# A long convolution and two expert layers: the expert matmuls read their moving columns in another order, and the weights start 48 bytes later

## The chip, the cores and the metric

The kernel runs on one core of one Trainium2 chip. What is measured is the device time of one execution in microseconds (us); of several executions the median is given. The engines are named as in the profile: PE is TensorE's matmuls, PEld its weight loads, DVE is VectorE, ACT is ScalarE, POOL is GpSimd, SP is SyncE, which starts most DMAs.

## The reference

What is computed is a gated long convolution followed by two expert layers, one after the other, over 2 x 12480 = 24960 tokens of 128 features:

```python
h_filt = (np.maximum(pos_emb @ w1, 0.0) @ w2) * np.exp(-0.01 * pos)[:, None]
u = x * v
y = np.fft.irfft(np.fft.rfft(u, n=L, axis=1) * np.fft.rfft(h_filt, n=L, axis=0), n=L, axis=1)[:, :S, :]
x = (x * y).reshape(B * S, D)            # D = 128
h = x @ w_in;   x = (h * np.cos(h)) @ w_out                      # first expert, d_ff = 2048
h = x @ w_in2;  return (h * np.clip(h + 3.0, 0.0, 6.0) / 6.0) @ w_out2   # second expert, d_ff = 2048
```

Inputs are float32, the expert weights arrive as float64 bits and are split in the kernel into a high and a low float32r part.

## The kernel before, in words

`conv_phase` (until about 545 us) computes the convolution as matrix products for the transform of length 111 x 113, two features at a time (64 groups), and writes the product x * y to DRAM scratch. Its matmuls are float32 (L280 and L281, two at a time, in the left and right columns of the array). Beside it `decode` turns the weights into their two parts, 512 columns at a time.

`moe_phase` (from there to the end) holds the tokens as columns. There are 49 tiles (`TILES`): 47 of 512 tokens, and a first and a last one of 448. For each tile and expert there are 8 units; a unit is 256 of the 2048 hidden features.

- `front` (L685 to L703) multiplies a unit's two blocks of 128 x 128 input weights with the tile's 512 columns. Values are split in two float32r parts, so each block takes three matmuls: high weights on the high part `xh`, high weights on the low part `xl`, low weights on `xh`. It makes 6 matmuls, into PSUM tiles `ha0` and `ha1` (first expert, one buffer) or `hb` (second expert, two buffers).
- `m1_reduce`, `m1_gate` and `m1_split` (first expert) bring h into range (ACT L710, DVE L711), take the cosine and multiply (ACT L720, DVE L721) and split the product into `hi` (ACT L728) and `lo` (POOL L733). `m2_gate` and `m2_split` (second expert) do the same with ACT L740, DVE L741 and L755, POOL L758.
- `back` (L760 to L783) multiplies the unit's two 128 x 128 blocks of output weights with `hi` and `lo`: 6 matmuls that add to `acc`, a PSUM tile that is open over the tile's 8 units. After the eighth, ACT L777 and DVE L778 split `acc` into `x2h` and `x2l`, the second expert's input; or ACT L782 copies it to `o`, and SP writes `o` to the output.

The order is written out by hand in the loop at L795: iteration p takes front(p) of the first expert, then back of an earlier unit of the first, then front of the second expert 12 iterations behind, then back of an earlier unit of the second. In the middle of the kernel an iteration is thus 24 matmuls, each with a weight load of its own. In all there are 2 x 2 x 6 x 8 x 49 = 9408 such matmuls (6 in front, 6 in back, two experts).

Every matmul of `front` and `back` takes its columns in the order in which they lie (L701 and L769, `rhs=r[:, :n]`), and all tiles that they read start at multiples of 64 bytes. Weights are the first 4096 floats of a tile per matrix (`weights`, L78), 2048 high and then 2048 low.

Of the kernel before, what the change touches and what calls it, by code (L numbers as in the profile page):

```python
# [10 lines left out]
F32R = mybir.dt.float32r  # L11
INT32 = mybir.dt.int32
UINT32 = mybir.dt.uint32
ACTF = mybir.ActivationFunctionType
ALU = mybir.AluOpType
# [13 lines left out]
MP = 2 * M2  # L29
# [4 lines left out]
DFF = 2048  # L34
# [2 lines left out]
TT = 512  # L37
XW = 4 * N2
LINE = 64
HB = -(-max(36 * MP, 2 * DFF) // LINE) * LINE  # L40
XB = -(-XW // LINE) * LINE
TILES = [(TT + TOK % TT) // 2] + [TT] * (TOK // TT - 1) + [(TT + TOK % TT) // 2]
TWO_PI = 2.0 * np.pi
# [3 lines left out]
def kernel(  # L47
# [19 lines left out]
    nc = tc.nc  # L67
    dram = ctx.enter_context(tc.tile_pool(name="dram", bufs=1, space=DRAM))
    wp = ctx.enter_context(tc.tile_pool(name="wp", bufs=1))
# [6 lines left out]
    hq = ctx.enter_context(tc.tile_pool(name="hq", bufs=1))  # L76

    def weights(e, nm):  # L78
        if (nm, e) not in w_hi:
            if e == 0:  # L80
                t = wp.tile([128, 2, DFF], F32R, name=f"w{nm}")
            else:
                t = hq.tile([128, HB], F32R, tag=f"h{'io'.index(nm)}", name=f"v{nm}")[:, :2 * DFF]
                t = t.rearrange("p (z f) -> p z f", f=DFF)
            w_hi[nm, e], w_lo[nm, e] = t[:, 0, :], t[:, 1, :]
        return w_hi[nm, e], w_lo[nm, e]

# [23 lines left out]
    def decode(task, st, pool, lane):  # L111
        e, nm, c = task
        lo, hi = st[:, :, 0], st[:, :, 1]
        ex = pool.tile([128, DC], INT32, tag=f"wex{lane}", name="wex")
        mh = pool.tile([128, DC], INT32, tag=f"wmh{lane}", name="wmh")
        m = mh.bitcast(FP32)
        wh, wl = (w[:, c:c + DC] for w in weights(e, nm))
        nc.vector.tensor_scalar(ex, hi, 9, 0x3FFFFF, op0=ALU.logical_shift_right, op1=ALU.bitwise_and)
        nc.vector.tensor_scalar(mh, hi, 0x1FF, None, op0=ALU.bitwise_and)
        yield  # L120
        nc.scalar.activation(out=ex, in_=ex, func=ACTF.Relu, bias=b_exp, scale=-1.0)
        nc.scalar.activation(out=ex, in_=ex, func=ACTF.Relu, bias=b_max, scale=-(2.0 ** 12))
        nc.scalar.activation(out=m, in_=mh, func=ACTF.Copy, scale=2.0 ** -20)
        yield
        nc.vector.scalar_tensor_tensor(
            out=ex, in0=hi, scalar=-0x80000000, in1=ex, op0=ALU.bitwise_and, op1=ALU.bitwise_or
        )
        yield
        nc.scalar.copy(wh, ex.bitcast(FP32))
        nc.vector.scalar_tensor_tensor(  # L130
            out=m, in0=lo.bitcast(UINT32), scalar=2.0 ** -52, in1=m, op0=ALU.mult, op1=ALU.add
        )
        yield
        nc.vector.tensor_scalar(ex, ex, -0x800000, None, op0=ALU.bitwise_and)
        yield
        nc.gpsimd.tensor_tensor(out=wl, in0=m, in1=ex.bitcast(FP32), op=ALU.mult)
# [497 lines left out]
    def moe_phase(mctx):  # L634
# [14 lines left out]
        acc = {}  # L649

        def n_of(t):
            return TILES[t]
# [15 lines left out]
        def split_x(t):  # L668
# [10 lines left out]
            eng.tensor_tensor(out=lo[:, :n], in0=f[:, :n], in1=hi[:, :n], op=ALU.subtract)  # L679
            xs[0, t] = (hi, lo)  # L680

        class Unit:
            pass

        def front(e, t, u, split):  # L685
            n = n_of(t)
            un = Unit()
            un.e, un.t, un.u, un.n = e, t, u, n
            xh, xl = xs[e, t]
            if split:  # L690
                hs = [ps_a.tile([128, 1, TT], FP32, tag=f"ha{c}", name=f"ha{c}") for c in range(2)]
                un.parts = [(slice(c, c + 1), hs[c][:, :, :n]) for c in range(2)]
            else:
                h = ps_b.tile([128, 2, TT], FP32, tag="hb", name="hb")
                hs = [h[:, c:c + 1] for c in range(2)]
                un.parts = [(slice(0, 2), h[:, :, :n])]
            for c in range(2):
                sl = slice((2 * u + c) * 128, (2 * u + c + 1) * 128)
                for k, (w, r) in enumerate(((w_hi, xh), (w_hi, xl), (w_lo, xh))):
                    nc.tensor.matmul(  # L700
                        out=hs[c][:, 0, :n], lhsT=w["i", e][:, sl], rhs=r[:, :n], start=(k == 0), stop=(k == 2)  # L701
                    )
            return un  # L703

# [55 lines left out]
        def back(un):  # L760
            e, t, u, n = un.e, un.t, un.u, un.n
            if u == 0:
                bank = 1 if t == 0 else e
                acc[e] = ps_o.tile([128, TT], FP32, tag=f"acc{bank}", name=f"acc{e}")
            for k, (w, r) in enumerate(((w_hi, un.hi), (w_lo, un.hi), (w_hi, un.lo))):
                for c in range(2):
                    sl = slice((2 * u + c) * 128, (2 * u + c + 1) * 128)
                    nc.tensor.matmul(  # L768
                        out=acc[e][:, :n], lhsT=w["o", e][:, sl], rhs=r[:, c, :n],  # L769
                        start=(u == 0 and c == 0 and k == 0), stop=(u == KFF // 2 - 1 and c == 1 and k == 2),  # L770
                    )
            if u == KFF // 2 - 1:
                a = acc[e][:, :n]
                if e == 0:
                    hi = x2_p.tile([128, TT], F32R, tag="x2h", name="x2h")
                    lo = x2_p.tile([128, TT], F32R, tag="x2l", name="x2l")
                    nc.scalar.copy(hi[:, :n], a)  # L777
                    nc.vector.tensor_tensor(out=lo[:, :n], in0=a, in1=hi[:, :n], op=ALU.subtract)  # L778
                    xs[1, t] = (hi, lo)
                else:  # L780
                    o = o_p.tile([128, TT], FP32, tag="o", name="o")
                    nc.scalar.activation(out=o[:, :n], in_=a, func=ACTF.Copy, scale=1.0 / 6.0)  # L782
                    nc.sync.dma_start(out=out_t[:, starts[t]:starts[t] + n], in_=o[:, :n])  # L783

        NU = KFF // 2
# [9 lines left out]
        for p in range(P2 + 3):  # L795
            if p < P1:
                t, u = divmod(p, NU)
                un = first[p] = front(0, t, u, p >= SHIFT or p % 3 == 0)
                un.alone = p < SHIFT
                m1_reduce(un)  # L800
                if u == 3:
                    load_x(t + 2)
                if u == 4:
                    split_x(t + 1)
# [12 lines left out]
            for q in (p - 4, p - 3):  # L817
                if q in first and first[q].alone == (q == p - 4):
                    back(first.pop(q))
            if SHIFT <= p < P2:  # L820
                second[p] = front(1, *divmod(p - SHIFT, NU), p == P2 - 1)
# [9 lines left out]
            if p - 3 in second:  # L831
                back(second.pop(p - 3))

    with tc.manual_schedule():
        nc.gpsimd.memset(b_exp, 1151.0 * 2.0 ** 11 - 1.0)
        nc.gpsimd.memset(b_max, 255.0 * 2.0 ** 23 - 2.0 ** 12)
        nc.gpsimd.memset(b_one, 1.0)
        nc.gpsimd.memset(bias3, 3.0)
        nc.gpsimd.memset(biaspi, float(np.pi / 2))
        nc.gpsimd.memset(biasq, 0.25)  # L840
        with ExitStack() as cctx:
            conv_phase(cctx)
        with ExitStack() as mctx:
            moe_phase(mctx)
# [96 lines left out]
```

## Time and profile before

| | |
|---|---|
| median of 3 runs | 2677.12 us (2676.82 to 2678.05) |
| the profiled execution's own time | 2676.21 us |
| its span in the profile | 2674.3 us |
| PE busy | 2655.9 us (99%) |
| PEld, POOL, DVE, ACT busy | 80%, 90%, 88%, 81% |

The span is the time from the first to the last instruction that the profiler recorded; the 1.9 us outside it are the start and the end of the program. Busy shares are the union of an engine's instructions. Matmuls overlap (one starts while the one before it drains), so a busy PE is not one at its peak: how fast it goes is read from the distance of the starts.

### The profile page before, as it was taken

Reading aid. Unit: us, or ns where it says so; the run is one execution under the profiler, and the core shown is the slowest. Engines: PE = TensorE matmul, PEld = TensorE weight load, DVE = VectorE, ACT = ScalarE, POOL = GpSimd, SP = SyncE. Lnnn points to the kernel's source line nnn. Section 1 sums busy time; section 2 is a strip of 40 time slices with the busy share of each in tenths; the row PEclk is TensorE's granted clock in tenths of the full one; section 3 lists DMA queues with packets and bytes.
Section 4 is the critical chain, followed back from the end, with each engine's and each line's share of the span. In section 5 each row is a group of like instructions: output and inputs, shape, how many; then the busy total and the mean of one; then the engine's idle time right before and its main releaser. Section 6 shows DMA issues by size and latency. Waiting matters only on the chain.

```text
span 2674.3 us, 45722 instructions
## 1 busy us (share of the span) xinstructions
PE 2655.9 (99%) x16362; PEld 2149.8 (80%) x16362; DVE 2343.5 (88%) x3188; ACT 2161.2 (81%) x3140; POOL 2398.6 (90%) x1321
## 2 busy tenths in 40 slices
PE   9999999989999999999999999999999999999999
PEld 6777777678888888888888888888888888888888
DVE  7999998788888888888888888888888888888887
ACT  5666665588888888888888888888888888888885
POOL 6999998789998989898999999898989899999987
PEclk9999999999999999999999999999999999999999
DMA  4443332200000000000000000000000000000000
GB/s 117 108 108 99 103 105 79 64 21 8 17 9 17 17 9 17 9 17 9 16 9 17 9 17 8 17 15 11 16 9 17 9 17 8 17 9 16 8 9 12
DMA packets 88312, 79.86 MB, mean 30 GB/s; under 512 B 57028, under 2 KB 78870, under 8 KB 88086
## 3 DMA queue, kind: packets, MB, share of 16 engines
q1 hardware_dynamic: 87790, 76.80, 10.6%
q8 instruction: 132, 2.16, 0.3%
q14 instruction: 94, 0.77, 0.1%
q10 hardware_dynamic: 296, 0.13, 0.0%
HBM read 51.15 MB, written 25.74 MB: 29 GB/s over the span
## 4 chain that ended last, share of the span: by engine, by line
PE 97%; ACT 1%; POOL 1%; DVE 1%; issue 0%; DMA 0%; SPq 0%; ACTq 0%; DVEq 0%; POOLq 0%
PE acc L768 39%; PE hb L700 20%; PE ha L700 19%; PE ap L281 5%; PE v L281 3%; PE xp L281 3%; PE bp L281 3%; PE xh L281 2%; PE ap L280 1%; PE hps L346 0%; PE bp L280 0%; PE rp L333 0%; ACT r L720 0%; ACT k L710 0%; POOL lo L733 0%
## 5 line engine op out<-in xcount | busy, mean ns | idle before, releaser
L758 POOL TENSOR_TENSOR lo<-g,hi 128x1024 fp32r<-128x1024 f32 (+1 forms) x390 | 938.1, 2406 | 195.4 <-PE ha L700 172.6
L733 POOL TENSOR_TENSOR lo<-g,hi 128x1024 fp32r<-128x1024 f32 (+1 forms) x392 | 941.6, 2403 | 2.8 <-ACT hi L728 2.0
L710 ACT ACTIVATE k<-ha,biasq 128x512 int32<-128x512 f32 (+1 forms) x768 | 501.6, 688 | 264.8 <-PE ha L700 258.5
L721 DVE TENSOR_TENSOR g<-ha,r 128x512 f32<-128x512 f32 (+1 forms) x768 | 499.8, 689 | 230.1 <-ACT r L720 230.0
L700 PE MATMUL hb<-x2h,vi 128*128 128x512 f32 (+1 forms) x1564 | 543.7, 388 | 0.0
L700 PE MATMUL ha<-xh,wi 128*128 128x512 f32 (+1 forms) x1524 | 530.6, 389 | 4.1 <-DVE g L721 4.1
L720 ACT ACTIVATE r<-r,biaspi 128x512 f32<-128x512 f32 (+1 forms) x776 | 520.7, 720 | 0.6 <-DVE r L711 0.4
L711 DVE SCALAR_TENSOR_TENSOR r<-k,ha 128x512 f32<-128x512 int32 (+1 forms) x768 | 488.7, 677 | 2.6 <-ACT k L710 2.3
L741 DVE SCALAR_TENSOR_TENSOR g<-q,hb 128x1024 f32<-128x1024 f32 (+1 forms) x391 | 472.3, 1208 | 7.9 <-ACT q L740 7.8
L755 DVE SCALAR_TENSOR_TENSOR hi<-q,hb 128x1024 fp32r<-128x1024 f32 (+1 forms) x390 | 469.9, 1205 | 0.0
L740 ACT ACTIVATE q<-hb,bias 128x1024 f32<-128x1024 f32 (+1 forms) x391 | 433.5, 1109 | 19.3 <-PE hb L700 18.4
L768 PE MATMUL acc<-hi,wo 128*128 128x512 f32 (+1 forms) x1568 | 418.4, 389 | 0.0
L768 PE MATMUL acc<-hi,vo 128*128 128x512 f32 (+1 forms) x1568 | 417.7, 388 | 0.0
L728 ACT CAST hi<-g 128x1024 fp32r<-128x1024 f32 (+1 forms) x385 | 401.4, 1043 | 0.0
L768 PEld LDWEIGHTS acc<-hi,wo 128*128 128x128 f32 x1568 | 294.8, 188 | 59.9
L768 PEld LDWEIGHTS acc<-hi,vo 128*128 128x128 f32 x1568 | 294.6, 188 | 59.6
L700 PEld LDWEIGHTS hb<-x2h,vi 128*128 128x128 f32 x1564 | 293.3, 188 | 60.2 <-issue 0.6
L700 PEld LDWEIGHTS ha<-xh,wi 128*128 128x128 f32 x1524 | 286.5, 188 | 63.9 <-issue 2.8
L700 PE MATMUL hb<-x2l,vi 128*128 128x512 f32 (+1 forms) x782 | 303.7, 388 | 0.0
L700 PE MATMUL ha<-xl,wi 128*128 128x512 f32 (+1 forms) x762 | 296.1, 389 | 0.0
L768 PE MATMUL acc<-lo,wo 128*128 128x512 f32 (+1 forms) x784 | 241.2, 389 | 0.4 <-DVE g L721 0.3
L768 PE MATMUL acc<-lo,vo 128*128 128x512 f32 (+1 forms) x784 | 240.7, 388 | 0.0
(155 smaller groups left out, 4078.3 us busy)
## 6 DMA issues: line engine op xcount, KB each, us to landing
x<-in_x_dram SPq DMA_DIRECT2D x64, 199.5 KB
v<-in_v_dram SPq DMA_DIRECT2D x64, 199.5 KB
scr<-z SPq DMA_DIRECT2D x128, 98.9 KB
out_dram<-o SPq DMA_DIRECT2D x47, 256.0 KB
xf<-scr SPq DMA_DIRECT2D x17, 256.0 KB
wst<-in_wi_dram SPq DMA_DIRECT2D x8, 512.0 KB
wst<-in_wo_dram SPq DMA_DIRECT2D x8, 512.0 KB
pt<-in_post_dram SPq DMA_DIRECT2D x14, 224.0 KB
```

The costliest lines, as they stand in the source:

```text
L281: nc.tensor.matmul(out=out[OD:m], lhsT=lhsT[:, OD:m], rhs=rhs if rhs2 is None else rhs2)
L700: nc.tensor.matmul(out=hs[c][:, 0, :n], lhsT=w["i", e][:, sl], rhs=r[:, :n], start=(k == 0), stop=(k == 2))
L710: nc.scalar.activation(out=k[:, c, :n], in_=h, func=ACTF.Identity, bias=biasq, scale=1.0 / TWO_PI)
L711: nc.vector.scalar_tensor_tensor(out=un.r[:, c, :n], in0=k[:, c, :n], scalar=-TWO_PI, in1=h, op0=ALU.mult, op1=ALU.add)
L720: nc.scalar.activation(out=rc, in_=rc, func=ACTF.Sin, bias=biaspi, scale=1.0)
L721: nc.vector.tensor_tensor(out=un.g[:, c, :n], in0=h, in1=rc, op=ALU.mult)
L733: nc.gpsimd.tensor_tensor(out=un.lo[:, :, :n], in0=un.g[:, :, :n], in1=un.hi[:, :, :n], op=ALU.subtract)
L740: nc.scalar.activation(out=un.r[:, c, :n], in_=h, func=ACTF.Relu, bias=bias3, scale=1.0)
L741: nc.vector.scalar_tensor_tensor(out=un.g[:, c, :n], in0=un.r[:, c, :n], scalar=6.0, in1=h, op0=ALU.min, op1=ALU.mult)
L755: nc.vector.scalar_tensor_tensor(out=un.hi[:, c, :n], in0=un.r[:, c, :n], scalar=6.0, in1=h, op0=ALU.min, op1=ALU.mult)
L758: nc.gpsimd.tensor_tensor(out=un.lo[:, :, :n], in0=un.g[:, :, :n], in1=un.hi[:, :, :n], op=ALU.subtract)
L768: nc.tensor.matmul(out=acc[e][:, :n], lhsT=w["o", e][:, sl], rhs=r[:, c, :n], start=(u == 0 and c == 0 and k == 0), stop=(u == KFF // 2 - ...
```

## The change

`front` and `back` now hand the matmul its moving columns through `taken`: of each 64 bytes (16 columns) first the first 16 bytes (4 columns), over the whole tile, then the second 16 bytes, and so on, in four passes. The outputs are written to PSUM in the order in which they come (`given` only gives the output the same shape). So each product stands in PSUM in the order in which it was taken, the elementwise work leaves it there, and `back` permutes once more; the three copies out of `acc` (L777, L778, L782) write 16-byte pieces to where the tokens belong (`twice`, `plain`). The order of the instructions, their number and their shapes stay as they are. Weight tiles of both experts start 12 floats (48 bytes) into their buffers, which are 64 floats longer for the first expert and as long as before for the second (4160 floats).

```diff
-HB = -(-max(36 * MP, 2 * DFF) // LINE) * LINE
+LEAD = 12
+Q4 = 4
+WB = -(-(LEAD + 2 * DFF) // LINE) * LINE
+HB = -(-max(36 * MP, WB) // LINE) * LINE
...
-                t = wp.tile([128, 2, DFF], F32R, name=f"w{nm}")
+                t = wp.tile([128, WB], F32R, name=f"w{nm}")
             else:
-                t = hq.tile([128, HB], F32R, tag=f"h{'io'.index(nm)}", name=f"v{nm}")[:, :2 * DFF]
-                t = t.rearrange("p (z f) -> p z f", f=DFF)
+                t = hq.tile([128, HB], F32R, tag=f"h{'io'.index(nm)}", name=f"v{nm}")
+            t = t[:, LEAD:LEAD + 2 * DFF].rearrange("p (z f) -> p z f", f=DFF)
...
+        def taken(r):
+            return r.rearrange("p (b a c) -> p a b c", a=Q4, c=Q4)
+        def given(o):
+            return o.rearrange("p (a b c) -> p a b c", a=Q4, c=Q4)
+        def twice(a):
+            return a.rearrange("p (m b c) -> p m b c", m=Q4 * Q4, c=Q4)
+        def plain(t):
+            return t.rearrange("p (b m c) -> p m b c", m=Q4 * Q4, c=Q4)
...
-                        out=hs[c][:, 0, :n], lhsT=w["i", e][:, sl], rhs=r[:, :n], start=(k == 0), stop=(k == 2)
+                        out=given(hs[c][:, 0, :n]), lhsT=w["i", e][:, sl], rhs=taken(r[:, :n]),
+                        start=(k == 0), stop=(k == 2),
...
-                        out=acc[e][:, :n], lhsT=w["o", e][:, sl], rhs=r[:, c, :n],
+                        out=given(acc[e][:, :n]), lhsT=w["o", e][:, sl], rhs=taken(r[:, c, :n]),
...
-                a = acc[e][:, :n]
+                a = twice(acc[e][:, :n])
...
-                    nc.scalar.copy(hi[:, :n], a)
-                    nc.vector.tensor_tensor(out=lo[:, :n], in0=a, in1=hi[:, :n], op=ALU.subtract)
+                    nc.scalar.copy(plain(hi[:, :n]), a)
+                    nc.vector.tensor_tensor(out=plain(lo[:, :n]), in0=a, in1=plain(hi[:, :n]), op=ALU.subtract)
...
-                    nc.scalar.activation(out=o[:, :n], in_=a, func=ACTF.Copy, scale=1.0 / 6.0)
+                    nc.scalar.activation(out=plain(o[:, :n]), in_=a, func=ACTF.Copy, scale=1.0 / 6.0)
```

## Rows read from the trace of the kernel before

**Rows 1.** Chain that ended last, from the page: shares of the span by engine

```profile
PE 97%; ACT 1%; POOL 1%; DVE 1%; issue 0%; DMA 0%; SPq 0%; ACTq 0%; DVEq 0%; POOLq 0%
```

**Rows 2.** Busy time by stretch: each engine's busy us and instructions, granted clock, DMA

```profile
1400.00:1800.00 400.00, 400.00 (x1766) 331.35 (x1765) 355.46 (x451) 347.14 (x470) 363.80 (x158) 1.00 0.05 13
1800.00:2200.00 400.00, 400.00 (x1766) 331.32 (x1765) 355.52 (x451) 346.92 (x469) 362.46 (x157) 1.00 0.05 14
```

**Rows 3.** PE in time, one iteration: start us, length us, instruction

```profile
1499.70 0.39 PE L700 MATMUL hb<-x2h,vi 128*128 128x512 f32 x1
...
1502.42 0.39 PE L700 MATMUL ha<-xh,wi 128*128 128x512 f32 x1
...
1505.14 0.39 PE L700 MATMUL hb<-x2h,vi 128*128 128x512 f32 x1
```

**Rows 4.** PE in time, 448-column matmuls of the last tile's first expert

```profile
2616.69 0.36 PE L700 MATMUL ha<-xh,wi 128*128 128x448 f32 x1
2616.89 0.37 PE L700 MATMUL ha<-xl,wi 128*128 128x448 f32 x1
2617.10 0.57 PE L700 MATMUL ha<-xh,wi 128*128 128x448 f32 x2
...
2619.12 0.39 PE L700 MATMUL hb<-x2h,vi 128*128 128x512 f32 x1
```

**Rows 5.** Line L768 from 2616.5 to 2621 us: ns min/median/max, first and last start

```profile
L768 PE MATMUL acc<-hi,wo x4: 365/365/369, 2617.9 to 2618.5; 128*128 128x448 f32 x4
L768 PE MATMUL acc<-hi,vo x3: 389/389/389, 2620.5 to 2621.0; 128*128 128x512 f32 x3
L768 PE MATMUL acc<-lo,wo x2: 362/366/369, 2618.7 to 2618.9; 128*128 128x448 f32 x2
```

**Rows 6.** Weight loads by shape: busy us and mean ns of one, then idle time before

```profile
L768 PEld LDWEIGHTS acc<-hi,vo 128*128 128x128 f32 x1568 | 294.6, 188 | 59.6
L280 PEld LDWEIGHTS xp<-at,cs 121*64 121x64 f32 x256 | 34.8, 137 | 1.2 <-DVE y L449 1.1
```

**Rows 7.** PE in time in the convolution: the pairs into xp, then into v

```profile
206.97 0.54 PE L281 MATMUL xp<-at,cs 121*49 121x448 f32 x1
...
208.47 0.55 PE L281 MATMUL v<-b,gm 112*48 112x456 f32 x1
208.49 0.55 PE L280 MATMUL v<-b,gm 112*64 112x456 f32 x1
...
210.03 0.26 PE L281 MATMUL ap<-f,hf 111*57 111x112 f32 x1
```

**Rows 8.** Waits from 600 to 2600 us: total, times, longest

```profile
ACT k L710 <- PE ha L700: 249.8, 324, 1.2
DVE g L721 <- ACT r L720: 223.1, 368, 1.1
POOL lo L758 <- PE ha L700: 170.4, 222, 1.3
```

**Rows 9.** All engines in time: when PSUM tile ha is released

```profile
1506.26 1.30 DVE L721 TENSOR_TENSOR g<-ha,r 128x512 f32<-128x512 f32 x2 [0.68 <-ACT r L720]
...
1507.86 0.39 PE L700 MATMUL ha<-xh,wi 128*128 128x512 f32 x1
```

**Rows 10.** The copies out of acc, by shape

```profile
L782 ACT ACTIVATE o<-acc 128x512 f32<-128x512 f32 x47 | 28.1, 598 | 8.0 <-PE acc L768 8.0
L777 ACT CAST x2h<-acc 128x512 fp32r<-128x512 f32 x47 | 26.9, 573 | 0.0
L778 DVE TENSOR_TENSOR x2l<-acc,x2h 128x512 fp32r<-128x512 f32 x47 | 32.0, 681 | 0.0
```

**Rows 11.** Two DVE products by shape: single floats 456 bytes apart, and runs

```profile
L356 DVE TENSOR_TENSOR h<-hps,win 111x144 f32<-111x144 f32 x56 | 16.8, 427 | 13.6 <-PE hps L346 13.6
L506 DVE TENSOR_TENSOR w<-vb,v2b 112x228 f32<-112x228 f32 x4 | 1.4, 390 | 1.3 <-ACT v2b L499 1.3
```

**Rows 12.** The end of the kernel in time

```profile
2670.24 0.57 PE L768 MATMUL acc<-lo,vo 128*128 128x448 f32 x2
2670.85 0.54 ACT L782 ACTIVATE o<-acc 128x448 f32<-128x448 f32 x1 [2.47 <-PE acc L768]
```

## The prediction, made before the changed kernel was run

> **What bounds the kernel now.** I read the chain that ended last first: PE holds 97% of it [rows 1], so what an edit is worth is read from PE's pace. Next the stretches: in the middle of the expert phase PE has no gap at all in 400 us, at the full granted clock of 1.00 (the 2.4 GHz level), and starts 1766 matmuls, one every 400 / 1766 = 0.2265 us [rows 2]. The timeline gives the same: an iteration of 24 matmuls runs from 1499.70 to 1505.14 us, 5.44 / 24 = 226.7 ns each [rows 3]. Streaming 512 columns at 2.4 GHz would take 213.3 ns. So every matmul holds 13.3 ns that are not its columns, and 9408 of them make 9408 x 13.3 ns = 125 us. That is all that any new reading order can win, and the question is what the 13.3 ns are.
>
> Two views speak on that. In the convolution a matmul with a weight load of its own has almost no such rest: four pairs into xp take 208.47 - 206.97 = 1.50 us, 375 ns each [rows 7], and 448 columns at half the rate are 373.3 ns; the rest is 1.7 ns. There the array takes a column only every second cycle and the weight load is 64 columns (137 ns) where an expert's is 128 (188 ns) [rows 6]. So a matmul with its load need not cost 13 ns; where the columns stream at full rate beside a full load it does. The second view is the 448-column matmuls. They should leave a constant rest, if it is a fixed price of the instruction; but their starts lie 200 and 210 ns apart at the beginning of one block [rows 4] (read to 10 ns), and their recorded lengths vary with the place in the sequence, 362 to 369 ns at the same line and shape, while the 512-column ones beside them have 389 each time [rows 5]. A rest that depends on the phase looks like two streams that meet: the moving columns of one matmul, and the weights for the next, which load at the same time. The weight load shows no loss (188 ns in each), so it is the moving stream that yields. That is an inference; no row shows the two apart.
>
> **The change, part by part.**
>
> *Moving columns in four passes, weights 48 bytes on (all 9408 matmuls).* The number of columns stays, and each 16-byte piece is still read whole, 4 columns at a time. What changes is where the pieces lie: in each quarter of a matmul all pieces have the same place within 64 bytes. A load reads 128 x 4 = 512 bytes in a row, 32 pieces that take the four places in turn. Of the 13.3 ns I leave 1.7 as the price that the convolution shows without contention; 11.6 ns are the meetings. How many of them the new order saves no row shows. From above: all, 9408 x 11.6 ns = 109 us. From the other side: none, or more than now, since the number of pieces that each stream reads is the same (the price of that is under the rivals). I take the middle model that the layout itself suggests: only weight pieces at the place at which the moving stream stays can meet it, one in four, so three quarters of the 11.6 ns go: 8.7 ns a matmul, 9408 x 8.7 = 82 us. A matmul would then start every 218.0 ns, and an iteration take 5.23 us.
>
> *How a read in short runs is priced.* The nearest row with a broken moving read is v: its 456 columns come in 8 runs of 57 with gaps. Four pairs take 210.03 - 208.47 = 1.56 us, 390 ns each [rows 7], 10 ns over the 380 ns of their columns at half rate, where xp has 1.7. So a break in the reading order cost 8.3 / 8 = 1.0 ns there. In the change a 512-column matmul has 127 breaks. From below a break costs nothing: v's runs of 228 bytes end in the middle of a 16-byte piece, the change's never do. I take nothing, as the pieces here are whole, and keep the 1.0 ns for the slower rival.
>
> The Trainium skill ("SBUF — State Buffer", under SBUF: two separate sides, the note on cachelines) bears on this: it says that reads are served in lines of 16 bytes and run at full bandwidth if at least two accesses fall on each line. By that rule four floats a line are free at any distance, and the sum stays as it is; v's extra 8.3 ns agree with it, as its runs leave lines with one float. No row here has whole lines apart from each other.
>
> *What PE's pace reaches.* If PE speeds up from 226.7 to 218.0 ns, the others must follow: it has 96.2% of the time. POOL was busy 363.80 of 400 us [rows 2], 91%, and would be 95%; DVE (355) 92%, ACT (347) 90%. None becomes the bound on average. In detail: ACT, DVE and POOL now wait 250, 223 and 170 us for others in 2000 us [rows 8]; 4% of 2000 us is 77 us, and each has that. The next thing late would be ha: its second half is released when DVE L721 ends at 1507.56, the first matmul that writes this half starts three matmuls after 1507.86, at 1508.54 [rows 9]: about 1.0 us of slack, 27 matmuls after the front before it began. These 27 become 27 x 8.7 = 235 ns shorter. It holds.
>
> *Copies out of acc.* ACT L777 and L782 and DVE L778 (49 each) write pieces of 16 bytes, 256 bytes apart; they took 573, 598 and 681 ns [rows 10]. The trace has no such write; the worst near row is DVE L356, which writes single floats 456 bytes apart, 427 / 144 = 2.97 ns an element where runs take 390 / 228 = 1.71 [rows 11]. So a copy costs between nothing and 512 x 1.26 = 0.65 us more; I take nothing, since runs of 4 floats are nearer to runs. At the worst ACT has 98 x 0.65 = 64 us and DVE 32 us more, inside waits of 250 and 223 us [rows 8]. What stands behind a late x2h is the second expert's front, 48 matmuls (10.5 us) after the last back of the first expert: covered. Only the last L782, after the last matmul [rows 12], is on the path: at most 0.57 us for its 448 columns.
>
> *Weight tiles 256 bytes longer, starts 48 bytes on.* The decode writes the same number of elements, no instruction and no DMA is added or passed: nothing.
>
> **Sum.** Profiled execution 2676.2 us (span 2674.3 and 1.9 outside it) less 82 is 2594; it lies 0.9 us under the median of the runs, so 2595 us by the median, and 0.6 more at the worst copy.
>
> **Rivals.**
> 1. *The rest is no meeting, or the new order meets as often.* 13.3 ns is then the price of changing weights at this rate, or a quarter of the moving stream beside a load that passes all four places collides as before. For it: 512-column matmuls have the same 226.7 ns at all lines and operands [rows 3, 5], which looks like a fixed price; against it the 448-column rows [rows 4, 5]. Time 2677 us, give or take 2. The Trainium skill says as much ("SBUF — State Buffer", Who interferes with whom): TensorE has two independent read ports, for moving columns and weight loads, and never waits on anyone. By that rule nothing is to be won; the varied lengths of rows 5 speak against it, though they don't refute it.
> 2. *A part is saved.* The phase decides: the load may shift so that it meets less often, but a quarter or half of the 11.6 ns remain saved at most. 9408 x 2.9 to 5.8 ns = 27 to 55 us: 2622 to 2650 us.
> 3. *Slower: a break in the reading order costs time at the moving port*, because one place visited over and over can't answer as fast as four in turn. Place: every expert matmul. Price: v's 1.0 ns a break would be 127 ns a matmul, +1195 us less the 82 gained, some 3790 us; a tenth of it still 12.7 ns, +119 - 82 = +37, 2714 us. It outweighs the gain from 8.7 / 127 = 0.07 ns a break. For it: v is the only row with breaks and it shows a price. Against it: v's ends are broken pieces, and its columns pass at half rate.
>
> **How the numbers follow.** Forecast (three quarters or all of the meetings go, 2565 to 2622 us): 0.42. Rival 2, down to a gain that just shows (2622 to 2671): 0.17. Rival 1: 0.18. Rival 3: 0.23, of which I put 0.08 below 2714. That makes faster 0.59, same 0.18, slower 0.23, where the same means within 0.2% (5.4 us), about what a measurement of this kernel can tell from no change. The likeliest case gives 2595 us. The range from 2558 (all 125 us would give 2552) to 2712 leaves out 0.02 below and 0.15 above; the likeliest case's own range is 2565 to 2622.
>
> **What would show it.** In the stretch from 1400 to 1800 us PE's count rises from 1766 to about 1835; an iteration of 24 matmuls is 5.23 us instead of 5.44; PEld's 188 ns stay; POOL, DVE and ACT rise to 95, 92 and 90%, and PE still has no wait for them. The rows of the convolution stay as they are. The forecast is wrong if the pace stays at 226.7 ns (rival 1), if it lies above it (rival 3: recorded matmul lengths over 389 ns), or if PE shows waits for ha, hi or lo. L777, L778 and L782 show the price of pieces: at or near 573, 681 and 598 ns.

## The result, and the profile after

The changed kernel takes 2617.39 us (median of 4 runs, 2617.22 to 2619.8) where the one before took 2676.97 in the same comparison: a ratio of 0.9779, 95% interval 0.9762 to 0.9796, or 59.6 us less. Forecast were 2595 us in a range of 2558 to 2712, so the direction and the range held, and the gain is 0.73 of the one forecast.

The first view is the busy time by stretch: us of each engine with its instructions, granted clock, share of the DMA engines, GB/s. PE starts 1818 matmuls in 400 us where it started 1766 [rows 2], at the same granted clock:

```profile
1400.00:1800.00 400.00, 400.00 (x1818) 340.69 (x1817) 365.45 (x465) 355.19 (x483) 372.39 (x162) 1.00 0.04 13
1800.00:2200.00 400.00, 400.00 (x1818) 340.71 (x1817) 365.87 (x464) 354.99 (x484) 373.63 (x162) 1.00 0.05 14
```

PE in time (start us, length us) shows one iteration of 24 matmuls, from the first row of hb at 1506.16 to the next at 1511.44 us: 5.28 us, 220 ns each, where it took 5.44 us, 227 ns each [rows 3]:

```profile
1506.16 0.38 PE L715 MATMUL hb<-x2h,vi 128*128 128x512 f32 x1
...
1507.48 1.04 PE L784 MATMUL acc<-hi,vo 128*128 128x512 f32 x4
...
1508.80 0.38 PE L715 MATMUL ha<-xh,wi 128*128 128x512 f32 x1
...
1510.12 1.04 PE L784 MATMUL acc<-hi,wo 128*128 128x512 f32 x4
...
1511.44 0.38 PE L715 MATMUL hb<-x2h,vi 128*128 128x512 f32 x1
```

In the starts as the trace holds them, in whole ns, nearly all of the 512-column matmuls (8710 of 9036) are exactly 220 ns apart. A weight load is still 188 ns; weight loads by shape (busy us, mean ns of one, idle time before), against [rows 6]:

```profile
L784 PEld LDWEIGHTS acc<-hi,vo 128*128 128x128 f32 x1568 | 294.3, 188 | 49.3
```

The other engines follow. Waits from 600 to 2550 us (total, times, longest), about as many matmuls as in the 2000 us of [rows 8]: ACT gave up 49 us, DVE 57, POOL 44, and PE waits for none of them.

```profile
ACT k L726 <- PE ha L715: 200.5, 325, 1.1
DVE g L737 <- ACT r L736: 166.4, 369, 0.8
POOL lo L774 <- DVE hi L771: 126.5, 231, 1.1
```

The three copies out of acc, in 16-byte pieces now, cost what they cost in runs [rows 10]:

```profile
L798 ACT ACTIVATE o<-acc 128x512 f32<-128x512 f32 x47 | 28.1, 597 | 4.4 <-PE acc L784 0.3
L793 ACT CAST x2h<-acc 128x512 fp32r<-128x512 f32 x47 | 26.9, 572 | 0.0
```

```profile
L794 DVE TENSOR_TENSOR x2l<-acc,x2h 128x512 fp32r<-128x512 f32 x47 | 32.0, 681 | 0.0
```

Where the 59.6 us come from: 226.67 - 220.0 = 6.67 ns, 16 cycles at 2.4 GHz, times 9408 is 62.7 us. Of these 4 us are lost again: the span in the trace is 58.6 us shorter. About 2 us go at the token tiles: as a new tile's first front begins, some matmuls in a row lie 225 to 235 ns apart, until the pace is back at 220 (here 1503.46 to 1504.61, 0.23 us apart; the kernel before has no such stretch between 627 and 2591 us):

```profile
1503.46 0.39 PE L715 MATMUL ha<-xh,wi 128*128 128x512 f32 x1
1503.69 0.39 PE L715 MATMUL ha<-xl,wi 128*128 128x512 f32 x1
1503.92 0.62 PE L715 MATMUL ha<-xh,wi 128*128 128x512 f32 x2
1504.38 0.39 PE L715 MATMUL ha<-xl,wi 128*128 128x512 f32 x1
1504.61 0.38 PE L715 MATMUL ha<-xh,wi 128*128 128x512 f32 x1
```

The other 2 us lie before 630 us, where PE still waits for others. There the granted clock fell once more than in the kernel before, to its lower level of 1.2 GHz from 573.4 to 576.8 us, after PE had waited 2.5 us for DVE L737; eight starts then lie 423 to 427 ns apart. The kernel before has a wait of 2.4 us at the same place and kept the upper level.

### The profile page after: what moved, and what is told of

Read it like the earlier page. It is cut to its first block, busy times and chain, and to the rows that moved or that the text cites. A ratio compares the mean times of both kernels' runs of the same rounds, so it can differ in the third digit from the quotient of the medians.

```text
span 2615.7 us, 45720 instructions
## 1 busy us (share of the span) xinstructions
PE 2598.3 (99%) x16362; PEld 2149.6 (82%) x16362; DVE 2344.5 (90%) x3188; ACT 2150.5 (82%) x3140; POOL 2394.7 (92%) x1321
## 4 chain that ended last, share of the span: by engine, by line
PE 97%; ACT 1%; POOL 1%; DVE 1%; DMA 1%; issue 0%; DVEq 0%; POOLq 0%; ACTq 0%; SPq 0%
PE acc L784 39%; PE hb L715 20%; PE ha L715 19%; PE ap L284 5%; PE v L284 4%; PE xp L284 3%; PE bp L284 3%; PE xh L284 2%; PE ap L283 1%; PE rp L336 1%; PE hps L349 0%; PE bp L283 0%; DMA x<-scr 0%; POOL lo L749 0%; ACT r L736 0%
## 5 line engine op out<-in xcount | busy, mean ns | idle before, releaser
L726 ACT ACTIVATE k<-ha,biasq 128x512 int32<-128x512 f32 (+1 forms) x768 | 494.6, 687 | 214.0 <-PE ha L715 208.5
L737 DVE TENSOR_TENSOR g<-ha,r 128x512 f32<-128x512 f32 (+1 forms) x768 | 500.0, 690 | 171.9 <-ACT r L736 171.7
L715 PE MATMUL hb<-x2h,vi 128*128 128x512 f32 (+1 forms) x1564 | 530.5, 379 | 0.0
L715 PE MATMUL ha<-xh,wi 128*128 128x512 f32 (+1 forms) x1524 | 519.5, 381 | 3.5 <-DVE g L737 3.5
L784 PE MATMUL acc<-hi,wo 128*128 128x512 f32 (+1 forms) x1568 | 406.7, 379 | 0.0
L784 PE MATMUL acc<-hi,vo 128*128 128x512 f32 (+1 forms) x1568 | 406.4, 379 | 0.0
L715 PE MATMUL hb<-x2l,vi 128*128 128x512 f32 (+1 forms) x782 | 296.5, 379 | 0.0
L715 PE MATMUL ha<-xl,wi 128*128 128x512 f32 (+1 forms) x762 | 290.3, 381 | 0.0
L784 PE MATMUL acc<-lo,wo 128*128 128x512 f32 (+1 forms) x784 | 235.0, 380 | 1.0 <-POOL lo L749 1.0
L784 PE MATMUL acc<-lo,vo 128*128 128x512 f32 (+1 forms) x784 | 235.1, 380 | 0.0
## 6 DMA issues: line engine op xcount, KB each, us to landing
pt<-in_post_dram SPq DMA_DIRECT2D x14, 224.0 KB
```

What stands on the lines that cost most here:

```text
L715: nc.tensor.matmul(out=given(hs[c][:, 0, :n]), lhsT=w["i", e][:, sl], rhs=taken(r[:, :n]), start=(k == 0), stop=(k == 2),)
L726: nc.scalar.activation(out=k[:, c, :n], in_=h, func=ACTF.Identity, bias=biasq, scale=1.0 / TWO_PI)
L737: nc.vector.tensor_tensor(out=un.g[:, c, :n], in0=h, in1=rc, op=ALU.mult)
L784: nc.tensor.matmul(out=given(acc[e][:, :n]), lhsT=w["o", e][:, sl], rhs=taken(r[:, c, :n]), start=(u == 0 and c == 0 and k == 0), stop=(u ...
```

## The experiments

The theory after the result: part of what a matmul holds over its 213.3 ns comes from meetings of its moving columns with the weights that load beside it, decided by the place of their 16-byte pieces within 64 bytes. The rivals: the start of the weights alone does it, or the reading order alone, or the rest is a fixed price. Single runs stand beside a run of the kernel before of 2676.5 to 2677.4 us; the pace comes from the starts of the 512-column matmuls.

**1. Each half of the change alone.** The order without the 48 bytes, and the 48 bytes without the order.

```diff
-LEAD = 12
+LEAD = 0
```

> The new reading order, weights at the start of their buffers as before (no 48 bytes). Theory (moving columns and weight load meet at the same place within 64 bytes, so the order does the work and the start of the weights only sets the phase): a matmul every 218 to 224 ns, 2600 to 2650 us. Rival (where the weights start does the work): 226.7 ns as before, about 2677 us.

```diff
-            return r.rearrange("p (b a c) -> p a b c", a=Q4, c=Q4)     # taken; given, twice and plain alike
+            return r
```

> The old reading order, weights 48 bytes on. Theory: the two streams each pass all four places in turn, a start one place later only shifts when they meet: 226.7 ns, 2677 us. Rival (the start of the weights does the work): 220.0 ns, about 2617 us.

Measured: 2674.92 us with the order alone, 2736.55 us with the lead alone. Busy time by stretch, first of the order alone, then of the lead alone:

```profile
1400.00:1800.00 400.00, 400.00 (x1767) 331.01 (x1766) 355.61 (x452) 347.20 (x470) 362.10 (x158) 1.00 0.05 13
```

```profile
1400.00:1800.00 400.00, 400.00 (x1716) 325.56 (x1715) 345.75 (x439) 341.47 (x456) 354.53 (x153) 1.00 0.05 13
```

By their starts the matmuls lie 226.7 and 233.3 ns apart. Neither half gains: the order alone is worth nothing (226.7 before, and 1.6 us of time), the lead alone costs 6.7 ns, both together save 6.7. Both rivals that name one half fall, and so does my theory as I had put it, which gave the gain to the order. With the order alone the pace isn't even constant: seven distances repeat, 226, 220, 222, 221, 234, 239 and 225 ns. The weights' addresses change the pace of the same moving reads, so the two streams do act on each other; what a single meeting is, no row shows.

**2. Other leads.** 16 and 32 bytes, and 112, which is 48 and 64.

```diff
-LEAD = 12
+LEAD = 4          # and 8, and 28
```

> The new reading order, weights 16 bytes on instead of 48. Theory: the phase of the meetings changes, 218 to 227 ns; if one in four weight pieces costs the same wherever it falls, 220.0 ns and 2617 us as with 48. Rival (the rest is a fixed price and the gain came from whole-line reading alone): exactly 220.0 ns.

> The new reading order, weights 32 bytes on. Theory: as with 16 bytes, 218 to 227 ns by phase; a different value from the others would show that the start matters beside the order. Rival: exactly 220.0 ns, 2617 us.

> The changed kernel with the weights 112 bytes on, which is 64 + 48. Theory (weight load and moving columns meet by their place within 64 bytes): the same as with 48, 220.0 ns a matmul, 2617 us. Rival (places repeat at 128 bytes or more, or the distance itself matters): another pace, 222 to 234 ns.

Measured: 2704.75, 2676.85 and 2664.89 us, at 230.0, 226.7 and 225.3 ns. Busy time by stretch, in that order:

```profile
1400.00:1800.00 400.00, 400.00 (x1740) 325.80 (x1740) 350.82 (x445) 343.94 (x463) 355.98 (x155) 1.00 0.05 13
```

```profile
1400.00:1800.00 400.00, 400.00 (x1766) 330.20 (x1765) 356.28 (x452) 346.78 (x470) 361.45 (x157) 1.00 0.04 13
```

```profile
1400.00:1800.00 400.00, 400.00 (x1777) 332.05 (x1776) 357.58 (x453) 348.58 (x473) 364.07 (x159) 1.00 0.05 14
```

The start decides between 220 and 230 ns at the same order; with 16 bytes the pace lies outside the 218 to 227 ns expected. And 112 bytes are not 48: the places don't repeat at 64 bytes. That premise of the theory falls.

**3. The moving tiles 16 bytes on, instead of the weights.** All tiles that a matmul streams begin 4 floats later, weights at 0.

```diff
-            un.hi = g_p.tile([128, 2, TT], F32R, tag="hi", name="hi")
+            un.hi = g_p.tile([128, 2 * TT + 16], F32R, tag="hi", name="hi")[:, MOVE:MOVE + 2 * TT].rearrange("p (z n) -> p z n", n=TT)
...
```

> The new reading order, weights at the start of their buffers, and instead every moving tile (xh, xl, x2h, x2l, hi, lo, x0h, x0l) 16 bytes on: the moving columns start one place ahead of the weights, as with weights 48 bytes on. Theory (only the place of one stream against the other counts): 220.0 ns, 2617 us. Rival (the weight load has an alignment of its own that it likes): about 226.7 ns as with the order alone, 2675 us, or something else.

Measured: 2669.39 us, 225.9 ns with no pattern that repeats. The expectation rested on the 64 bytes and fell with them. As the longer buffers also began at multiples of 64 instead of 256 bytes, this run alone tells little; experiment 5 does it cleanly.

**4. Weights at one place.** Each block's 128 weight columns stand 64 bytes apart, the block's number choosing the place; in the new order and in the old.

```diff
-                        ... lhsT=w["i", e][:, sl], ...
+                        ... lhsT=w["i", e].rearrange("p (m j) -> p j m", j=KFF)[:, 2 * u + c, :], ...
```

> The new reading order, and weights stored so that each block of 128 columns is read with a step of 64 bytes, all at one place: place 0 for units 0 and 1, place 1 for units 2 and 3, 2 for 4 and 5, 3 for 6 and 7 (the decode writes them there). Theory: the moving stream is at places 0, 1, 2, 3 in its four quarters, and the load falls in the first half or more of a matmul: units at place 3 meet nothing and take 213 to 217 ns, units at place 0 or 1 meet in a whole quarter and take more than 220. Rival (the rest is a fixed price): all units alike. A second rival (a load of single floats costs more by itself): all units slower alike, weight loads over 188 ns.

> Weights stored as in the kernel before this one (each block at one place, step 64 bytes), moving columns in the old order, which passes all four places every 16 columns. Theory: every unit meets its place once in four pieces, all places alike up to phase: one pace for all units, between 216 and 235 ns. Rival (fixed price): 226.7 ns.

Measured: 2690.52 and 2775.28 us, 227.2 and 236.8 ns a matmul. A load of single floats takes 297 to 302 ns instead of 188, as the second rival had it. Loads now overlap each other and PEld is busy 400 of 400 us; whether that sets the pace is not shown, since nearly the same loads go at two paces. But the units are not alike, as that rival and the expectation of the old order had them. In the new order the means of a unit's matmuls go from 222.4 to 237.5 ns, and units 6 and 7, at place 3, which were to take 213 to 217, have 222 to 238; in the old order they go from 234.4 to 240.7, with units 6 and 7 together the slowest in all four matrices. So the weights' place counts here too, and not by the theory. Weight loads by shape, the new order:

```profile
L787 PEld LDWEIGHTS acc<-hi,wo 128*128 128x128 f32 x1568 | 385.3, 299 | 0.3
L787 PEld LDWEIGHTS acc<-hi,vo 128*128 128x128 f32 x1568 | 382.7, 297 | 0.0
```

**5. Two sweeps of the moving tiles' start.** The start moves by 16 bytes on every third token tile, weights at 0, buffers 256 bytes longer so that all begin at multiples of 256; in the new order and in the old. That gives 16 starts in one run.

```diff
+        def move(t):
+            return 4 * min(t // 3, 15)
...
-                hi = x_p.tile([128, TT], F32R, tag="xh", name="xh")
+                hi = x_p.tile([128, TT + 64], F32R, tag="xh", name="xh")[:, move(t):move(t) + TT]
...
```

> A sweep in one run. The new reading order, weights at the start of their buffers, and the moving tiles start 16 bytes further on every third token tile, from 0 to 240 bytes (16 starts, three tiles each; their buffers are 256 bytes longer). Theory as mended by the earlier runs (what counts is the start of the moving columns against that of the weights, and the places repeat at 256 bytes, not at 64): a start of 208 bytes is the changed kernel (weights 48 bytes ahead, 256 - 48) and shows 220.0 ns; 240 bytes shows 230, 224 bytes 226.7, 144 bytes 225.3, 0 bytes 226.6, as the runs with weights 16, 32, 112 and 0 bytes on. With places that repeat at 128 bytes 80 and 208 would both show 220.0 and 16 and 144 both 225.3. Rival (the weights' own alignment counts): 226 to 227 ns at all starts.

> The sweep of 16 starts of the moving tiles (0 to 240 bytes, three token tiles each, weights at the start of their buffers), now in the old reading order. Theory (two streams meet, and order and start together set how often): the pace varies with the start; 226.7 ns at 0 bytes as in the kernel before, 233.3 at 208 bytes as with the weights 48 bytes on. What is open is how low it goes: if the order is needed for 220.0 ns, no start comes below some 224; if a start alone is enough, one start shows 220 or less, and the reading order was not needed. Rival (the old order passes all places so fast that the start is nothing): 226.7 ns at all starts.

Measured, the mean distance of starts in ns in the middle of each three tiles (about 180 matmuls, where both experts have the same start; at 0 bytes all lie in the beginning, and the mean is of 54 undisturbed ones):

| start, bytes | 0 | 16 | 32 | 48 | 64 | 80 | 96 | 112 | 128 | 144 | 160 | 176 | 192 | 208 | 224 | 240 |
|---|---|---|---|---|---|---|---|---|---|---|---|---|---|---|---|---|
| new order | 226.1 | 224.4 | 225.4 | 222.2 | 228.3 | 230.0 | 224.0 | 224.2 | 230.0 | 222.3 | 226.2 | 223.4 | 226.7 | 220.1 | 226.7 | 230.0 |
| old order | 226.7 | 231.6 | 233.3 | 233.3 | 233.3 | 231.1 | 233.3 | 231.1 | 232.3 | 233.3 | 234.3 | 233.3 | 233.3 | 234.7 | 233.3 | 233.3 |

Three of these stretches in the new order, starts 208, 224 and 240 bytes (the first 40.00 us with 184 matmuls, the second with 178, the third 41.00 us with 180):

```profile
2281.00:2321.00 40.00, 40.00 (x184) 34.09 (x183) 36.42 (x47) 36.05 (x50) 37.25 (x17) 1.00 0.04 11
2410.00:2450.00 40.00, 40.00 (x178) 33.01 (x177) 35.49 (x46) 35.21 (x49) 36.55 (x17) 1.00 0.04 11
2541.00:2582.00 41.00, 41.00 (x180) 33.68 (x179) 35.52 (x47) 35.69 (x50) 36.61 (x17) 1.00 0.02 7
```

In the old order, 208 bytes:

```profile
2331.00:2373.00 42.00, 42.00 (x181) 33.72 (x180) 35.63 (x47) 36.29 (x50) 37.29 (x17) 1.00 0.04 11
```

208, 224 and 240 bytes gave 220.1, 226.7 and 230.0, the values of weights 48, 32 and 16 bytes on: with 256 bytes as the distance at which places repeat, that is the same start of one stream against the other, reached from the other side. 80 and 208, which 128 bytes would make equal, gave 230.0 and 220.1. But the start of one stream against the other is not all. Two predicted values missed: 144 bytes in the new order (222.3 for 225.3) and 208 in the old (234.7 for 233.3). The means agree where the single distances don't: at 240 bytes 235 and 225 ns take turns, with weights 16 bytes on 226, 233, 234, 227 repeat. And at 96 bytes two paces follow each other, 220.0 ns from 1366 to 1398 us and 229 to 234 before and after; a start doesn't fix the pace alone.

The second row answers whether the order was needed. The old order shows 231 to 235 ns at every start but its own, 0, where it has 226.7 as in the kernel before. Over the 15 other starts its mean is 233.0 ns, that of the new order 225.6. So the order saves 7.4 ns on average, but the kernel before stood on the old order's best start, and the new order's start had to be chosen too: at 0 it has no better pace than the old one (experiment 1).

**6. A sweep of reading orders,** weights 48 bytes on, five token tiles each.

```diff
+        ORDERS = ((4, 4), (1, 4), (2, 4), (8, 4), (16, 4), (2, 8), (4, 8), (8, 8), (4, 16))
...
+        def taken(r, t):
+            a, c = order(t)
+            return r.rearrange("p (b a c) -> p a b c", a=a, c=c) if a > 1 else r
```

> A sweep in one run, weights 48 bytes on. The reading order changes with the token tile (five tiles each): the changed kernel's (16 bytes of each 64), the old one, 16 of each 32, 16 of each 128, 16 of each 256, 32 of each 64, 32 of each 128, 32 of each 256, 64 of each 256 bytes; tokens of all but the first are left in the order in which they come, so those columns of the output are not the reference's. Theory (the weights' pieces meet the moving ones by order and phase): the first 220.0 ns, the old order 233.3 as with 48 bytes alone, the others anywhere from 216 to 240, by phase; orders that stay longest away from the weights' place come lowest. Rival (runs that are broken cost time at the moving port): the shorter the pieces and the larger the step, the slower, 16 of each 256 slowest, above 233.

Measured in ns, in that order: 220.2, 233.3, 231.1, 242.9, 278.7, 232.0, 233.3, 244.7, 233.3. Stretches of the first, the old order, 16 bytes of each 128, and 16 of each 256:

```profile
632.00:757.00 125.00, 125.00 (x570) 106.51 (x569) 114.20 (x146) 111.52 (x153) 116.78 (x51) 1.00 0.05 13
849.00:980.00 131.00, 131.00 (x564) 106.56 (x563) 112.75 (x144) 112.59 (x152) 116.87 (x51) 1.00 0.04 12
...
1297.00:1434.00 137.00, 137.00 (x566) 107.52 (x565) 115.67 (x145) 113.78 (x152) 116.92 (x51) 1.00 0.05 12
1537.00:1695.00 158.00, 158.00 (x569) 108.83 (x568) 118.74 (x146) 119.38 (x153) 123.03 (x51) 1.00 0.03 11
```

None of the eight others beats the changed one at this start; at other starts they were not run. 16 bytes of each 256, the order in which all pieces of a pass have one place if places repeat at 256 bytes, is the slowest, 45 ns over the old order, or 0.36 ns for each of 128 pieces: an order can cost as much as the slower rival of the prediction feared, but with steps of 128 (242.9) and 256 bytes, not of 64. Whether that is a price of the moving reads themselves or more meetings with the loads is not shown, as no run has these orders without the loads. The order of the expectation's rival (shorter pieces, larger step, slower) holds for the steps over 64 bytes and not for the changed order; three paces lie over the 216 to 240 ns that the theory allowed.

**7. Half of the weight load.** Back's matmuls load 64 columns instead of 128 (the kernel leaves out half of the output features), front's stay whole; token tiles up to 23 in the old order, the others in the new.

```diff
+                    m = 128 if u == c == k == 0 or (u == KFF // 2 - 1 and c == 1 and k == 2) else 64
...
-                        out=given(acc[e][:, :n]), lhsT=w["o", e][:, sl], rhs=taken(r[:, c, :n]),
+                        out=given(acc[e][:m, :n], t), lhsT=w["o", e][:, sl][:, :m], rhs=taken(r[:, c, :n], t),
```

> Weights 48 bytes on; token tiles 1 to 23 in the old reading order, from tile 24 on in the new one. In back, all matmuls but the first and the last of an acc tile load only 64 of the 128 weight columns (half of the output features is left out; front keeps whole loads). Theory (what a matmul holds over its 213.3 ns comes from the pieces of the weight load that meet the moving stream): it halves with the load, seen between the six matmuls of one back: from 233.3 to about 223 ns in the old order, from 220.0 to about 217 in the new. Rival (it is a price of the moving stream's own reading or of the instruction): 233.3 and 220.0 ns stay. A change of the load's width between front and back may cost time of its own, seen only at the first matmul of each.

Measured: in the old order 226.7 ns between back's matmuls with half a load (means of 226.3 to 226.8 between the second and the fifth) and 233 between front's with a whole one (232.5 to 233.8); in the new order 219.3 to 220.0 in back, 220.6 to 221.6 in front. PE in time, first an iteration in the old order (back from 1001.58 to 1002.95, front from there to 1004.35), then one in the new:

```profile
1001.58 1.08 PE L790 MATMUL acc<-hi,vo 128*64 128x512 f32 x4
1002.49 0.62 PE L790 MATMUL acc<-lo,vo 128*64 128x512 f32 x2
1002.95 0.39 PE L720 MATMUL ha<-xh,wi 128*128 128x512 f32 x1
...
1004.12 0.40 PE L720 MATMUL ha<-xh,wi 128*128 128x512 f32 x1
...
2006.55 1.04 PE L790 MATMUL acc<-hi,vo 128*64 128x512 f32 x4
2007.43 0.60 PE L790 MATMUL acc<-lo,vo 128*64 128x512 f32 x2
2007.87 0.38 PE L720 MATMUL ha<-xh,wi 128*128 128x512 f32 x1
```

In the old order four half-load matmuls take 0.91 us, 227.5 ns each, and five whole-load ones 1.17 us, 234 each; in the new order four take 0.88 us, 220 each. So in the old order half of the load takes 6.7 ns off, of the 20.0 that a matmul holds there: the load is what costs them, on average one cycle of 2.4 GHz (0.42 ns) for each of the 16 pieces left out. That is less than the half that the theory expected (223 ns). In the new order half of the load takes at most 0.7 ns off the changed kernel's 220.0, where 217 ns were expected: at this start the 16 pieces left out cost little or nothing. What the 16 that are still loaded cost, no run shows.

## Why the prediction was right, and where its step was off

- **The bound.** PE's pace set the time before and sets it after; no other engine took over, and the slack of the others was as worked out (POOL at 93%, forecast 95 at a somewhat higher pace). Shown by the profile after.
- **That the rest comes from two streams that meet.** Right for a part: that the loads act on the moving reads is shown, as the pace of the same reads changes with the weights' start (experiments 1 and 2) and in the old order with the size of the load (experiment 7). That it is single 16-byte pieces that meet is argued.
- **The size of that part.** Here the sum was mis-sized. I left 1.7 ns as the price without meetings, from the pairs into xp [rows 7], and 11.6 as meetings, and let three quarters of these go: 8.7 ns. The runs put it otherwise: 6.7 ns went and 6.7 ns stay, in the new order with a whole load or with half of one. So of the 13.3 ns of before at least 6.7 depended on where the two streams lie. No steady pace in the runs came near the 1.7 ns of the xp pairs, which stream at half the rate. Whether the 6.7 ns that stay are a fixed price is not shown: single distances of 218 ns stand in the sweep (experiment 5, 112 bytes).
- **"Only weight pieces at the place at which the moving stream stays can meet it, one in four".** This model failed: by it the order would gain by itself. The order alone gained nothing, and places don't repeat at 64 bytes (2664.89 us with the lead at 112 bytes, 2617 at 48). What holds: order and start together set the pace, from 220.0 ns to 234.7 at steps of up to 64 bytes, and the kernel before stood in the middle, 226.7. That 220.0 is no piece of the load met and 233.3 all 32 (213.3 + 6.7 + 32 x 0.42) fits experiment 7 but is not shown; 234.7 is over it.
- **What was luck.** The forecast came within 23 us of the result by two errors that work against each other: 11.6 ns of meetings for 6.7 was too much, three quarters for all of the 6.7 too little (three quarters of 6.7 ns would be 47 us). The model behind the three quarters gives the gain to the order, and the order alone has none. And 2617 us lie 5 us from 2622, where the case of rival 2, a smaller part, began.
- **The lead of 48 bytes as a detail.** I priced it together with the order and gave it no term of its own; the line on the weights' starts in the sum, "nothing", looks at the decode and the DMAs alone. Yet the order gains nothing without it: then the time is 2675 us, and rival 1's number would have come true.
- **Rival 1 and its rule.** The Trainium skill ("SBUF — State Buffer", Who interferes with whom) has TensorE's two read ports independent and TensorE waiting on no one. Against other engines no run here speaks against it; between its own two reads the measurement does: the weights' start alone moved the pace by 6.7 ns (experiment 1).
- **Rival 3 and the lines of 16 bytes.** The same page (the Trainium skill, "SBUF — State Buffer", SBUF: two separate sides) lets whole lines be read at full rate. At 64 bytes the trace agrees, 220 ns. With a step of 256 bytes, still in whole lines and beside the weight loads, it does not: 278.7 ns (experiment 6). The Trainium skill has a penalty there for accesses that cross to a new line; weights read one float to a line agree, 297 to 302 ns for 188 (experiment 4).
- **Copies, convolution.** As forecast: 572, 681 and 597 ns for 573, 681 and 598; the pairs into xp and v start as before, v's at 208.47 us.

What stays open: by what rule order and start choose the pace (several starts repeat patterns of two to fourteen distances, and 96 bytes holds two paces), why 144 bytes in the new order and 208 in the old missed, and the 6.7 ns. Whether the token tiles' disturbed stretches can be had back was not tried. No run beat the changed kernel.

## What to carry to other kernels

Where every matmul has a weight load of its own, compare the distance of starts with columns / clock before touching anything: a rest that changes with addresses can be won in part by layout alone; here it took the reading order and the start of the weights together, so test them as a pair and sweep the start in one run by giving token tiles different starts. A price taken from a stage that streams at half the rate (1.7 ns) need not be the floor of one at the full rate (6.7 here). When one half of a change gains nothing alone, that says nothing about the pair.

## What the runs showed of the hardware that was not expected

- The start of the weights alone, with no instruction changed, moves a kernel's time from 2617 to 2705 us at one reading order (48 and 16 bytes).
- A matmul of 512 columns with a 128-column load was never steady below 220.0 ns, 528 cycles at 2.4 GHz, in any of 9 orders and 16 starts, though single ones came 218 ns after the one before; in the old order its mean went up to 234.7.
- Pieces of 16 bytes, 256 bytes apart, beside the weight loads cost 0.36 ns each more than in sequence (278.7 and 233.3 ns a matmul); a weight load with a step of 64 bytes takes 297 to 302 ns in place of 188.
